# Two attention blocks on one core: loads tied to exponentials, whole products for the first values, normalisation from a copy

## The chip, the cores and the metric

The kernel runs on one core of a Trainium2 chip (trn2). The metric is the time of one execution on the device in microseconds (us); the median of three runs is given. One execution was also taken with the hardware profiler: its page and its trace are what is quoted here.

The engines are PE (TensorE; PEld are its weight loads), ACT (ScalarE), DVE (VectorE), POOL (GpSimd) and SP (SyncE, which here only issues DMAs). L776 means line 776 of the kernel. A row of the timeline gives start, duration, engine, line, operation, output and input, the count, and in brackets the idle time before it with what ended it.

## What is computed

Two multi-head attentions over 2048 tokens of width 1024 (32 heads of 32), each with its own input and weights; the outputs lie side by side.

```python
def _A_ref(x, wqkv, wo):                      # full attention
    q, k, v = split(x @ wqkv)                 # 32 heads x 2048 x 32
    p = softmax(q @ k.T * Dh ** -0.5)
    return (p @ v) @ wo

def _B_ref(x, wq, wk, wv, wo, beta):          # 4 segments of 512 with a memory
    q, k, v = x @ wq, x @ wk, x @ wv
    for s in range(4):
        p = softmax(qs @ ks.T * scale + mask)               # causal in the segment
        num, den = phi(qs) @ M, phi(qs) @ z + 1e-06          # phi(t) = t + 1 or exp(t)
        o = g * num / den + (1 - g) * (p @ vs)               # g = sigmoid(beta)
        M, z = M + phi(ks).T @ vs, z + sum(phi(ks))
    return concat(o) @ wo
```

## The kernel before

**Tiling.** Heads go in groups of four (8 groups), since four heads of 32 fill 128 rows. In attention A a unit is a group g and a block c of 256 queries; it has 32 score tiles of 512 columns. In attention B a unit is a segment s and a group j. `pack` joins two or three tiles to one exponential on ScalarE of up to 1536 columns; there are 828 of them, and their order is fixed by the list of units in `plan` (`PAIR`, `B_FIRST`, `B_STEP`, `B_GAP` say how units of A and B are mixed). Two slots of three PSUM banks (0 to 2 and 3 to 5) take the scores in turn, so the scores of exponential n wait until exponential n - 2 has left its banks. Four buffers per slot hold the results P.

**What goes around an exponential.** `plan_op` makes its scores (L761: 32-row products of keys and queries) and the exponential (L776), whose bias is a bound on the scores that is worked out from the squares of keys and queries (`guard_cols`, `guard_end`; the tile dg is a diagonal that spreads the columns' maxima by a product with ones). `plan_pv` adds P times the values (L825) and P times ones (L831, the row sums) into bank 7, the only bank for that (`OL_BANKS`). When a unit's last tile is in, `norm` and `recip_rows` on DVE transpose the row sums (L849), take the reciprocal (L856), transpose back (L858) and multiply the values' sums by it (L903, L919, L915 or L898). Projections and output products are jobs of eight products each in bank 6, the only bank for those (`X_BANKS`); their results are copied out by DVE (L979, L1174, L1193, L1207, L1303).

**The order.** The whole program is a list of operations with keys (planned times) and due times. `Prog.schedule` puts them into one order per engine by a list of costs; PE takes the scores when they are due and fills the rest with sums and jobs by rank (`HEAT`, `STICK`, `OVER`, `AHEAD`, `JOB_AT`, `DUE_SLOPE` and others). Each engine then runs its list in order and waits on semaphores.

**The start.** SP loads A's input transposed in six pieces (`X_PIECES`, L959), ScalarE's queue loads the first key and query weights. `plan_prologue` projects keys and queries of the first 512 tokens (`quarter`), which alternates keys and queries in eight steps, copies them out (L1103, L1105), squares them (L1141) and forms the first bias. The first units run in parts (`PARTS`): part 0 has the first quarter's keys, part 1 the second quarter's, part 2 the rest; each has a bias of its own, and partial sums are rescaled (L880, L884). The values of the first pair of groups are made by `job_V0`: for each of two halves (groups 0 and 1) and four quarters of tokens, 32 products of 128 columns, each as four quarter products of 32 output rows by `mm4`:

```python
def mm4(self, e, out, w, x, start, stop):
    for t in range(4):
        r = slice(32 * t, 32 * t + 32)
        ins = e.matmul(out[r], w[:, r], x, start=start, stop=stop, tile_position=(0, 32 * t), skip_group_check=True)
```

**Loads.** Weights come by `load_WA`, `load_WAv`, `load_WB`, `load_WBv`, `load_WoA`, B's input by `load_xB`, all issued by SP through `dma`. They wait only for the tile that they overwrite to be free, and for their place in SP's order.

**The end.** For the last two blocks of 256 queries of A, output products of seven of the eight groups are made ahead (`job_part`, L1382) and the eighth is added when the last unit is normalised (`job_last`, L1400, L1402), ScalarE and DVE copying two tiles each.

Of the kernel before, what the change touches and what calls it, by code (L numbers as in the profile page):

```python
# [7 lines left out]
ALU = mybir.AluOpType  # L8
AX = mybir.AxisListType

P = 128
# [3 lines left out]
D = 1024  # L15
NG = 8
NSEG = 4
L = 512
SCALE = DH ** -0.5

QC = 256
# [6 lines left out]
PAIR = ((6, 0), (6, 1), (6, 2), (7, 0), (7, 1), (7, 2), (6, 3), (6, 4), (7, 3), (7, 4), (6, 5), (7, 5), (6, 6), (7, 6), (6, 7),  # L28
# [6 lines left out]
B_FIRST, B_STEP, B_GAP = 8.5, 1.3, 3.0  # L35
B_STEP3 = 1.2
# [26 lines left out]
def mark(rs, *tag):  # L63
    for r in rs:
        r.tag = tag
# [71 lines left out]
HEAT = 0.55  # L137
STICK = 0
OVER = 0.3
# [3 lines left out]
MARGIN = 0.5  # L143
RXJ = 4
LEAD_A, LEAD_B, DUE_AT, DUE_SLOPE = 15.0, 15.0, 8.0, 0.3
# [273 lines left out]
class _Kernel:  # L419
# [34 lines left out]
    def dma(self, fn, sem, key, reads=(), writes=(), issue=0.65, lat=3.0, eng="SP"):  # L454
        return self.pg.op(eng, fn, issue, key, reads, writes, sem=sem, lat=lat)

    def build(self):
        nc = self.nc
        with ExitStack() as es:
            self.es = es  # L460
            self.alloc()
            self.items = []
            self.plan()
# [30 lines left out]
    def alloc(self):  # L494
# [16 lines left out]
        self.r_WAv = Res()  # L511
# [71 lines left out]
        self.sm_WAv = self.sem("d_WAv")  # L583
# [129 lines left out]
    def plan_op(self, take, cols, T, slot):  # L713
# [15 lines left out]
        def f(key):  # L729
# [48 lines left out]
            a.prog = True  # L778
            b = 0
# [62 lines left out]
    def recip_rows(self, src, rsrc, n, key, add=None):  # L842
# [6 lines left out]
        self.dve(lambda e: e.transpose(T1[:, 0:n], src), n, key, rsrc, [r1])  # L849
# [8 lines left out]
        self.dve(lambda e: e.transpose(T2[:, 0:n].rearrange("p (b r) -> p b r", r=32), bc), n, key, [rr], [r2])  # L858
# [8 lines left out]
    def norm(self, t, key):  # L867
# [21 lines left out]
        else:  # L889
            lsrc, ro = self.ps[:, lcol:lcol + QC], [ob]  # L890
        if kind == "A":
            T2, r2 = self.recip_rows(lsrc, ro, QC, k)
# [15 lines left out]
        else:  # L908
            T2, r2 = self.recip_rows(lsrc, ro, QC, k)
# [4 lines left out]
            if t["s"] == 0:  # L914
                self.dve(lambda e: e.scalar_tensor_tensor(out=dst, in0=osrc, scalar=gcol, in1=T2[:, 0:QC], op0=ALU.mult,  # L915
                                                          op1=ALU.mult), QC, k, [ob, r2, self.r_g], rds)
            else:
                holds(rds, "mem", t["s"])
                self.dve(lambda e: e.scalar_tensor_tensor(out=T2[:, 0:QC], in0=osrc, scalar=gcol, in1=T2[:, 0:QC], op0=ALU.mult,  # L919
                                                          op1=ALU.mult), QC, k, [ob, r2, self.r_g], [r2])  # L920
# [4 lines left out]
    def load_WA(self, g, kq, key, eng="SP"):  # L925
# [5 lines left out]
                 lat=3.5, eng=eng)  # L931

    def load_WAv(self, g2, key, eng="SP"):
        mark([self.r_WAv], "W", g2)
        src = self.A_wqkv.rearrange("(i p) n -> p i n", p=P)[:, :, 2 * D + 256 * g2:2 * D + 256 * g2 + 256]
        self.dma(lambda e: e.dma_start(self.WAv[:, :, :], src), self.sm_WAv, key, [], [self.r_WAv], lat=4.8, eng=eng,
                 )
# [117 lines left out]
    def plan_prologue(self):  # L1055
# [17 lines left out]
        def loads(key):  # L1073
            for kq in range(2):
                self.load_WA(0, kq, key, eng="ACT")
            for n, (h, lo, hi, issue, lat) in enumerate(X_PIECES):
# [4 lines left out]
                if n == 1:  # L1081
                    self.load_WAv(0, key)
# [479 lines left out]
```

## Time and profile before

| | |
|---|---|
| median of 3 runs | 1206.79 us (1205.52 to 1206.8) |
| the profiled execution | 1208.03 us, its span 1206.3 us |
| ACT busy | 1168.2 us, 97% of the span |
| PE busy | 1132.0 us, 94% |
| DVE busy | 562.1 us, 47% |
| POOL busy | 216.0 us, 18% |
| chain that ended last | ACT 58%, PE 32%, DVE 6%, issue 3% |
| DMA | 65.73 MB, mean 54 GB/s |

The span runs from the first to the last instruction. The chain that ended last is followed back from the last instruction, at each step to what released it or to the instruction before it on its engine. Matmul ends are modelled, so a busy PE need not be PE at its peak. The page's DMA line cuts the span into 40 equal slices of 30 us, each digit the busy share of the DMA engines in tenths.

### The profile page before, as it was taken

How to read it: one execution, taken by the hardware profiler on the slowest of the kernel's cores; microseconds unless marked ns; L12 is line 12 of the kernel's file. 1: busy time of each engine (PE TensorE's matmuls, PEld its weight loads, DVE VectorE, ACT ScalarE, POOL GpSimd, SP SyncE). 2: the span in 40 equal slices, each digit the busy share in tenths (PEclk: the TensorE clock that was granted, in tenths of full speed). 3: DMA queues.
4: the chain of work that ended last, by engine and by line, in shares of the span. 5: the costliest groups of instructions: out<-in, count | busy, mean ns of one | idle time of the engine just before them, and what ended most of it. 6: DMA issues, size and time to landing. Idle time of an engine off the chain costs nothing.

```text
span 1206.3 us, 54054 instructions
## 1 busy us (share of the span) xinstructions
PE 1132.0 (94%) x25352; PEld 554.6 (46%) x25352; DVE 562.1 (47%) x1268; ACT 1168.2 (97%) x868; POOL 216.0 (18%) x279
## 2 busy tenths in 40 slices
PE   7999999999999999899999999989999999988998
PEld 4455444464444444365444444544444444433444
DVE  2353444444443465645634566375425563643223
ACT  4999999999999999999999999999999999999997
POOL 1210131302120222211201331222002230100000
PEclk9999999999999999999999999999999999999999
DMA  9701331412111223103211123002022410100101
GB/s 198 190 19 43 85 77 40 85 23 64 44 33 46 64 53 80 31 7 66 64 44 33 34 66 77 17 22 48 29 75 59 146 25 7 33 20 24 38 24 46
DMA packets 162159, 65.73 MB, mean 54 GB/s; under 512 B 131728, under 2 KB 159120, under 8 KB 161936
## 3 DMA queue, kind: packets, MB, share of 16 engines
q1 hardware_dynamic: 159568, 61.50, 21.0%
q8 instruction: 198, 3.24, 1.1%
q10 hardware_dynamic: 2368, 0.79, 0.3%
q14 instruction: 25, 0.20, 0.1%
HBM read 39.00 MB, written 11.73 MB: 42 GB/s over the span
## 4 chain that ended last, share of the span: by engine, by line
ACT 58%; PE 32%; DVE 6%; issue 3%; SPq 1%; DMA 1%; DVEq 0%; ACTq 0%
ACT P L776 56%; PE ps L451 16%; PE ps L761 7%; PE ps L825 5%; PE ps L831 4%; ACT PKQ_B L1228 1%; DVE T L849 1%; SPq L959 1%; DVE PKQ_B L1233 1%; DVE T L858 1%; DMA xT_A<-in_A_x_dram 1%; DVE T L919 0%; DVE cols L1001 0%; DVE PKQ_B L1230 0%; DVE KQ_A L979 0%
## 5 line engine op out<-in xcount | busy, mean ns | idle before, releaser
L776 ACT ACTIVATE P<-ps,bias 128x1536 bf16<-128x1536 f32 (+3 forms) x828 | 1148.1, 1601 | 20.3 <-PE ps L761 10.9
L831 PE MATMUL ps<-P,onesb 128*32 128x256 bf16 (+1 forms) x4864 | 301.4, 272 | 1.2 <-issue 1.2
L761 PE MATMUL ps<-KQ_A 32*128 32x256 bf16 x4096 | 276.8, 274 | 21.1 <-ACT P L776 18.5
L825 PE MATMUL ps<-P,V_A 128*32 128x256 bf16 x4096 | 260.5, 276 | 6.3 <-ACT P L776 1.7
L761 PEld LDWEIGHTS ps<-KQ_A 32*128 32x128 bf16 x4096 | 80.9, 92 | 236.1 <-issue 123.4
L451 PE MATMUL ps<-xT_A,W_A 128*32 128x512 bf16 x2048 | 145.6, 387 | 7.2 <-DVE KQ_A L979 2.0
L451 PE MATMUL ps<-xT_B,W_B 128*32 128x512 bf16 x2048 | 145.5, 382 | 6.0 <-DVE OT_B L1254 1.3
L831 PEld LDWEIGHTS ps<-P,onesb 128*32 128x32 bf16 x4864 | 131.9, 97 | 32.0 <-issue 1.9
L825 PEld LDWEIGHTS ps<-P,V_A 128*32 128x32 bf16 x4096 | 110.0, 97 | 66.5 <-issue 33.7
L985 POOL TENSOR_TENSOR sqB<-KQ_B 128x512 bf16<-128x512 bf16 x64 | 66.9, 1045 | 368.6 <-DVE KQ_B L979 350.3
L788 POOL TENSOR_SCALAR_AFFINE_SELECT P<-P 128x768 bf16<-128x768 bf16 (+2 forms) x128 | 80.8, 654 | 253.0 <-ACT P L776 252.8
L985 POOL TENSOR_TENSOR sqA<-KQ_A 128x512 bf16<-128x512 bf16 x60 | 63.3, 1055 | 248.0 <-DVE KQ_A L979 218.6
L1303 DVE CAST outsb<-ps 128x512 bf16<-128x512 f32 x56 | 38.6, 690 | 134.7 <-PE ps L451 134.6
L849 DVE STREAM_TRANSPOSE T<-ps 128x256 f32<-128x256 f32 (+1 forms) x148 | 72.4, 489 | 59.4 <-PE ps L831 46.3
L979 DVE CAST KQ_B<-ps 128x512 bf16<-128x512 f32 x64 | 44.2, 690 | 116.3 <-PE ps L451 110.8
L979 DVE CAST KQ_A<-ps 128x512 bf16<-128x512 f32 x60 | 41.3, 688 | 102.2 <-PE ps L451 102.1
L451 PE MATMUL ps<-Wv_A,xT_A 128*32 128x256 bf16 (+1 forms) x2560 | 74.2, 252 | 5.8 <-issue 3.4
L858 DVE STREAM_TRANSPOSE T<-rc 128x256 f32<-128x256 f32 (+1 forms) x152 | 73.6, 485 | 3.9
L451 PE MATMUL ps<-Wv_B,xT_B 128*32 128x512 bf16 x1024 | 71.7, 382 | 2.9 <-DVE cols L1001 1.6
L451 PEld LDWEIGHTS ps<-xT_A,W_A 128*32 128x32 bf16 x2048 | 46.0, 96 | 60.9 <-issue 23.3
L451 PE MATMUL ps<-Wo_B,OT_B 128*32 128x512 bf16 x1024 | 72.5, 382 | 0.5 <-DVE outsb L1303 0.3
L451 PEld LDWEIGHTS ps<-xT_B,W_B 128*32 128x32 bf16 x2048 | 44.9, 96 | 56.3 <-issue 28.0
(88 smaller groups left out, 779.1 us busy)
## 6 DMA issues: line engine op xcount, KB each, us to landing
Wv_B<-in_B_wv_dram SPq DMA_DIRECT2D x8, 1024.0 KB, 5.9
W_B<-in_B_wk_dram SPq DMA_DIRECT2D x32, 256.0 KB, 3.0
W_B<-in_B_wq_dram SPq DMA_DIRECT2D x32, 256.0 KB, 3.0
out_dram<-outsb SPq DMA_DIRECT2D x56, 128.0 KB, 1.8
W_A<-in_A_wqkv_dram SPq DMA_DIRECT2D x14, 256.0 KB, 3.0
ot_a_scratch<-OTst SPq DMA_DIRECT2D x51, 64.0 KB, 1.6
xT_A<-ot_a_scratch SPq DMA_DIRECT2D x6, 512.0 KB, 7.0
Wv_A<-in_A_wqkv_dram SPq DMA_DIRECT2D x4, 512.0 KB, 4.9
```

What stands on the lines that cost most here:

```text
L451: ins = e.matmul(out[r], w[:, r], x, start=start, stop=stop, tile_position=(0, 32 * t), skip_group_check=True)
L761: ins = e.matmul(out, kap, qap, start=st, stop=True, tile_position=(32 * h, 0), skip_group_check=True)
L776: a = self.act(lambda e: e.activation(dst, src, ACT.Exp, bias=self.bias[:, bc:bc + 1], scale=SCALE), cols, key, res + [self.r_bias[bc]], [rP])
L788: self.pool(lambda e, v=v, pat=pat: e.affine_select(v, v, pattern=pat, compare_op=ALU.is_ge, fill=0.0, base=0, channel_multiplier=-1), (m ...
L825: ins = e.matmul(self.ps[32 * h:32 * h + 32, 512 * obk + q0:512 * obk + q0 + nq], vt[:, c0 + 32 * h:c0 + 32 * h + 32], Pt[:, b, off:off + nq],
L831: ins = e.matmul(self.ps[32 * h:32 * h + 32, lcol + q0:lcol + q0 + nq], self.onesb[:, 0:32], Pt[:, b, off:off + nq], start=False, stop=las ...
L849: self.dve(lambda e: e.transpose(T1[:, 0:n], src), n, key, rsrc, [r1])
L858: self.dve(lambda e: e.transpose(T2[:, 0:n].rearrange("p (b r) -> p b r", r=32), bc), n, key, [rr], [r2])
L959: return self.dma(lambda e: e.dma_start(dst, src, transpose=True), sem, key, reads, writes, issue=issue, lat=lat)
L979: self.dve(lambda e: e.tensor_copy(dst, out), ncol, key + 1.0, [self.bank[b]], rdst)
L985: self.pool(lambda e: e.tensor_tensor(sq[:, :], src, src, ALU.mult), 512, key, [rsrc], [rs], rate=0.5)
L1303: self.dve(lambda e: e.tensor_copy(ob[:, :], self.ps[:, 512 * b:512 * b + 512]), 512, key + 1.0, [self.bank[b]], [ro])
```

## The change

Seven edits:

- `dma` takes a flag `gate`. With it the DMA also waits for the last exponential whose planned time is not after the DMA's key. All weight loads, B's input, beta and B's output weights use it. The planner's cost of issuing a DMA goes from 0.65 to 0.4.
- B's first input is planned at 30 instead of 4 (`RX0`), beta at 60 instead of 20, B's output weights at 200 instead of 100.
- `job_V0` makes each product whole (128 output rows, one weight load and one matmul) instead of four quarter products; the planner knows this as a third mode of PE, "full".
- The first pair's value weights come in two halves, the second half ahead of the last piece of A's input.
- In `recip_rows` DVE copies the values' sums from PSUM to SBUF right behind the first transpose (`keep`), and the multiplication reads that copy. Partial units and the very last unit have no such copy.
- `quarter` does four steps of keys, four of queries, then again four and four.
- Constants of the planner change: the mix of units and the ranks of jobs. The changed program has the same ScalarE instructions in the same sizes, 123 more copies on DVE, and 256 whole products on PE where 1024 quarter products stood.

```diff
+PAIR = (... (6, 3), (7, 3), (6, 4), (7, 4) ...)          # was (6, 3), (6, 4), (7, 3), (7, 4)
-B_FIRST, B_STEP, B_GAP = 8.5, 1.3, 3.0
-B_STEP3 = 1.2
+B_FIRST, B_STEP, B_GAP = 10.0, 1.25, 3.0
+B_STEP3 = 1.15
...
-HEAT = 0.55
-STICK = 0
-OVER = 0.3
+HEAT = 0.6
+STICK = 0.5
+OVER = 0.4
...
-MARGIN = 0.5
+MARGIN = 1
+RX0 = 30.0
-LEAD_A, LEAD_B, DUE_AT, DUE_SLOPE = 15.0, 15.0, 8.0, 0.3
+LEAD_A, LEAD_B, DUE_AT, DUE_SLOPE = 15.0, 12.0, 8.0, 0.5
...
-    def dma(self, fn, sem, key, reads=(), writes=(), issue=0.65, lat=3.0, eng="SP"):
-        return self.pg.op(eng, fn, issue, key, reads, writes, sem=sem, lat=lat)
+    def dma(self, fn, sem, key, reads=(), writes=(), issue=0.4, lat=3.0, eng="SP", gate=False):
+        o = self.pg.op(eng, fn, issue, key, reads, writes, sem=sem, lat=lat)
+        n = bisect.bisect_right(self.exp_keys, key)
+        if gate and n:
+            o.deps.add(self.exps[n - 1])
+        return o
...
-    def recip_rows(self, src, rsrc, n, key, add=None):
+    def recip_rows(self, src, rsrc, n, key, add=None, keep=None):
...
+        if keep is not None:
+            self.dve(lambda e: e.tensor_copy(T2[:, n:2 * n], keep), n, key, rsrc, [r2])
...
+        keep = osrc if t["part"] is None and (kind, g, t["c"]) != ("A", 7, 7) else None
+        T2, r2 = self.recip_rows(lsrc, ro, QC, k, keep=keep)
+        if keep is not None:
+            osrc, ro = T2[:, QC:2 * QC], []
...
-                if n == 1:
-                    self.load_WAv(0, key)
+                if n in (1, 4):
+                    self.load_WAv(0, key, n // 4, n // 4 + 1)
...
-            for i in range(8):
-                for kq in range(2):
+            for i, kq in [(i, kq) for lo in (0, 4) for kq in range(2) for i in range(lo, lo + 4)]:
...
-        self.item(20.0, beta)
+        self.item(60.0, beta)
...
-                o = self.pe(lambda e, i=i, t=t, k=k: self.mm4(
-                    e, self.ps[:, 512 * b + P * k:512 * b + P * k + P], self.xT[:, i, P * t:P * t + P],
-                    self.WAv[:, i, P * half:P * half + P], i == 0 and k == 0, i == 7), 0.0565, key,
-                    [self.r_WAv, self.r_xT[i][c]], [self.bank[b]])
+                o = self.pe(lambda e, i=i, t=t, k=k: e.matmul(
+                    self.ps[:, 512 * b + P * k:512 * b + P * k + P], self.xT[:, i, P * t:P * t + P],
+                    self.WAv[:, i, P * half:P * half + P], start=i == 0 and k == 0, stop=i == 7, skip_group_check=True), 0.058, key,
+                    [self.r_WAv[half], self.r_xT[i][c]], [self.bank[b]], mode="full")
...
-        self.item(100.0, lambda key: self.dma(... self.WoB ... lat=12.0))
+        self.item(200.0, lambda key: self.dma(... self.WoB ... lat=12.0, gate=True))
...
-                end, rx = 10.0, 4.0
+                end, rx = 10.0, RX0
...
-                r = max(en["B", s - 1, 4 * hh + 3] + 12.0, rx + 12.0) if s else 16.0
+                r = max(en["B", s - 1, 4 * hh + 3] + 12.0, rx + 12.0) if s else rx + 12.0
```

More of the change, by code (lines that the diff above doesn't have):

```diff
@@ L778, in f @@
             a.prog = True
+            self.exps.append(a)
+            self.exp_keys.append(key)
             b = 0
@@ L1176, in job_V0 @@
     def job_V0(self, half, c, key, bank=None, behind=None, copy_behind=None):
-        holds([self.r_WAv], "W", 0)
+        holds([self.r_WAv[half]], "W", 0)
         holds([r[c] for r in self.r_xT], "x")
```

51 lines of the change are left out of this document (25 added, 26 removed).

## The prediction

> **What bounds the kernel now.** I read the page first, then ScalarE's instructions in order of time, then PE and DMA where ScalarE idles, then how the built program of the change stands on each engine.
>
> ```profile
> span 1206.3 us, 54054 instructions
> PE 1132.0 (94%) x25352; PEld 554.6 (46%) x25352; DVE 562.1 (47%) x1268; ACT 1168.2 (97%) x868; POOL 216.0 (18%) x279
> DMA  9701331412111223103211123002022410100101
> q8 instruction: 198, 3.24, 1.1%
> ```
>
> ScalarE is busy for 1168.2 of 1206.3 us, nearly all of it in 828 exponentials. The changed program has the same ScalarE instructions in the same sizes, so the change can move only its 38.1 us of idle time. Here is most of that (in brackets the idle time before a row, and what ended it):
>
> ```profile
> 15.14 3.17 ACT L776 ACTIVATE P<-ps,bias 128x1536 bf16<-128x1536 f32 x2 [3.57 <-PE ps L451]
> 19.05 5.08 ACT L776 ACTIVATE P<-ps,bias 128x1536 bf16<-128x1536 f32 x4 [0.73 <-PE ps L761]
> 26.52 1.54 ACT L776 ACTIVATE P<-ps,bias 128x1536 bf16<-128x1536 f32 x1 [2.40 <-PE ps L451]
> 31.06 1.54 ACT L776 ACTIVATE P<-ps,bias 128x1536 bf16<-128x1536 f32 x1 [1.39 <-PE ps L761]
> 34.37 1.54 ACT L776 ACTIVATE P<-ps,bias 128x1536 bf16<-128x1536 f32 x1 [1.77 <-PE ps L761]
> 36.09 11.74 ACT L776 ACTIVATE P<-ps,bias 128x1536 bf16<-128x1536 f32 x8 [0.18 <-PE ps L761]
> ...
> 70.41 26.78 ACT L776 ACTIVATE P<-ps,bias 128x1536 bf16<-128x1536 f32 x19 [1.73 <-PE ps L831]
> 98.30 2.97 ACT L776 ACTIVATE P<-ps,bias 128x1536 bf16<-128x1536 f32 x2 [1.12 <-PE ps L761]
> ...
> 101.47 7.38 ACT L776 ACTIVATE P<-ps,bias 128x1536 bf16<-128x1536 f32 x5 [0.20 <-PE ps L761]
> 109.25 1.54 ACT L776 ACTIVATE P<-ps,bias 128x1536 bf16<-128x1536 f32 x1 [0.40 <-PE ps L761]
> 110.96 1.54 ACT L776 ACTIVATE P<-ps,bias 128x1536 bf16<-128x1536 f32 x1 [0.17 <-PE ps L761]
> 113.10 8.79 ACT L776 ACTIVATE P<-ps,bias 128x1536 bf16<-128x1536 f32 x6 [0.59 <-PE ps L761]
> ...
> 449.17 6.84 ACT L776 ACTIVATE P<-ps,bias 128x1536 bf16<-128x1536 f32 x5 [1.19 <-PE ps L761]
> 478.95 1.54 ACT L776 ACTIVATE P<-ps,bias 128x1536 bf16<-128x1536 f32 x1 [0.72 <-PE ps L761]
> 481.53 1.54 ACT L776 ACTIVATE P<-ps,bias 128x1536 bf16<-128x1536 f32 x1 [1.04 <-PE ps L761]
> ...
> 516.82 25.22 ACT L776 ACTIVATE P<-ps,bias 128x1536 bf16<-128x1536 f32 x19 [0.37 <-PE ps L761]
> ...
> 1085.30 10.70 ACT L776 ACTIVATE P<-ps,bias 128x1536 bf16<-128x1536 f32 x8 [0.36 <-PE ps L761]
> 1096.79 100.17 ACT L776 ACTIVATE P<-ps,bias 128x1536 bf16<-128x1536 f32 x72 [0.79 <-PE ps L831]
> 1201.71 1.08 ACT L1400 ACTIVATE KQ_B<-ps 128x512 bf16<-128x512 f32 x2 [4.75 <-PE ps L451]
> ```
>
> About 15 us pass before the first exponential and 9 after the last; 10.7 lie in the gaps shown up to 113 us, and 4.5 in those shown after it. Each gap ends on PE. PE's rows at the early ones:
>
> ```profile
> 13.14 1.07 PE L451 MATMUL ps<-Wv_A,xT_A 128*32 128x128 bf16 x64
> 14.03 0.39 PE L451 MATMUL ps<-dg,onesf 128*32 128x128 f32 x8
> 26.29 1.95 PE L451 MATMUL ps<-Wv_A,xT_A 128*32 128x128 bf16 x126
> 30.45 0.23 PE L451 MATMUL ps<-Wv_A,xT_A 128*32 128x128 bf16 x2 [2.21 <-issue]
> 69.73 0.29 PE L825 MATMUL ps<-P,V_A 128*32 128x256 bf16 x4 [0.49 <-DVE V_A L1193]
> 97.20 0.29 PE L831 MATMUL ps<-P,onesb 128*32 128x256 bf16 x4 [1.21 <-issue]
> 108.21 0.23 PE L451 MATMUL ps<-Wv_A,xT_A 128*32 128x128 bf16 x2 [0.73 <-issue]
> 30.70:34.20 3.50, 2.95 (x32) 0.90 (x32) 0.69 (x1) 1.54 (x1) 0.00 (x0) 0.65 1.25 275
> 444.60:448.10 3.50, 3.46 (x74) 2.23 (x78) 2.63 (x7) 3.38 (x3) 0.00 (x0) 0.52 0.19 37
> ```
>
> "issue" is time for which PE waited on nothing recorded, and it lies in or just behind the first pair's value products (L451, Wv_A, 128 columns). These use four quarter products for each whole one: 128 matmuls and 128 weight loads in 1.95 us. The 3.24 MB of the instruction queue over 50,704 PE instructions are 64 bytes each, its 198 packets 256 instructions each, so that stretch eats one packet in 1.95 us. I read the stalls as late instructions. The last two rows are windows (third number from the end: granted clock): after a stretch in which PE does little, the clock falls to about half for some 3.4 us, and ScalarE gaps (34.37, 449.17) follow.
>
> **The change part by part.** I count exponentials from 0.
>
> *Whole products, late bias.* In the order of before, half of the first value job stands ahead of the bias sum (dg) and half behind it; in the changed order all 32 whole products stand ahead. If a whole product takes what four quarters take, 1.07 / 16 = 67 ns, they end at 13.14 + 2 x 1.07 = 15.28. The first exponential stood 15.14 - 14.03 = 1.11 behind dg, so it starts at 16.4, 1.25 late. The six exponentials of the first quarter last 3.17 + 5.08 = 8.25, to 24.6. The next bias sum is queued behind scores 7, which wait for exponential 5 to free its banks: 0.35 for the scores, 1.11 for the chain, so exponential 6 starts near 26.1 instead of 26.52: **-0.4**. Keys ahead of queries bring the keys' copy out four products earlier and let it run beside the queries' products; that takes one copy of 512 columns (an estimate of 0.7, from 0.42 for 256 columns in a row below) off the chain whose bias sum started at 26.52 - 1.11 = 25.4, so its column is ready near 24.7, 0.3 before scores 7 let it through. So that edit is worth nothing while scores 7 cover it, and its absence about 0.4.
>
> For the whole product's price I take 67 ns because the same bits are streamed; the bounds are half of it (which gains 0.3, since the next column is then late) and 67 plus a wholly exposed 128-column weight load:
>
> ```profile
> L761 PEld LDWEIGHTS ps<-KQ_A 32*128 32x128 bf16 x4096 | 80.9, 92 | 236.1 <-issue 123.4 <-ACT P L776 108.7 <-DVE V_A L1193 0.4
> ```
>
> 67 + 92 = 159 ns makes 5.1 us for 32: exponential 0 at 19.3, and exponential 10 three to four us later than below. [...] No run here shows whole products yet.
>
> *The stall behind exponential 7.* The value job of the second quarter falls from 256 instructions to 64, a quarter packet; I let the 2.21 us stall go, and with it the half clock behind it. Exponentials 8, 9, 10 then follow without the gaps of 1.39, 1.77 and 0.18: **-3.3**. What is late next: 32 x 67 ns = 2.1 us of products before scores 8, which the two exponentials ahead (26.78 / 19 = 1.4 each) cover.
>
> *70 us.* The exponential at 70.41 waits for a value-sum of exponential 25, which in before stands behind scores 33 and a value copy; in the changed order it stands ahead of scores 32, and beta's casts are no longer between. **-1.5** of 1.73.
>
> *97 to 113 us.* Gaps of 1.12, 0.20, 0.40, 0.17 and 0.59, all beside the remaining quarter-product jobs: 2.48 in all, **-2.2**, leaving 0.3 for PE's mode changes.
>
> *Gated loads.* Every load of weights and second input now waits on SP for a named exponential; stores and transposes behind it in SP's queue wait too, which their rings of three and four buffers bear. Counting exponentials between a load's gate and its first product in PE's order, the time to spare is 3.1 us at the least and mostly 5 to 15, against:
>
> ```profile
> DMA to landing us min/median/max: 2.8/3.0/7.8
> ...
> 212.41 5.18 SPq L959 DMA_TRANSPOSE xT_B<-in_B_x_dram  x1
> 218.25 0.43 SPq L950 DMA_DIRECT2D Wv_B<-in_B_wv_dram  x1
> Wv_B<-in_B_wv_dram SPq DMA_DIRECT2D x1, 1024.0 KB, 7.8
> Wv_B<-in_B_wv_dram SPq DMA_DIRECT2D x8, 1024.0 KB, 5.9
> ```
>
> (first row: W_B loads after 60 us; the last two: value weights, that of 218.25 and the median of all). One place does not fit. At exponential 180 the second segment's input and its 1 MB of value weights are released together, and the key weights follow behind them, wanted ahead of scores 190, about 9.1 us after the gate. Issue of the input takes 5.2, so the value weights go at 5.8 and land at 11.7 to 13.6, the key weights behind them at about 12 to 14.5. ScalarE is fed until 12.0 if they land by 11.1, so it loses 0.8 to 3.5 there, and PE, idle for some 4 us, gets the half clock behind it, about 0.8 more. Bounds 0.5 and 5; I take **+2.5**. Before the change this input came with 49 exponentials to spare.
>
> *The rest up to the end.* Light stretches in PE's order (five exponentials with PE's sums and products under about a third of the time) stood at exponentials 295, 335, 685, 745 and 820 in before; the gaps at 449, 516 and 1085 to 1096 us lie right behind three of them. After the change, other than 185, they stand at 412, 508, 546, 590 and 817. About as many: 4.5 us of gaps become 3.7, **-0.8**, with bounds of 3 on both sides. In this lies the extra copy:
>
> ```profile
> L849 DVE STREAM_TRANSPOSE T<-ps 128x256 f32<-128x256 f32 x124 | 55.3, 446 | 47.3 <-PE ps L831 46.3
> ...
> 1199.94 0.42 DVE L898 TENSOR_TENSOR xT_A<-ps,T 128x256 bf16<-128x256 f32 x1
> ```
>
> The second row reads the same tile as the copy will: 123 copies of about 0.42 us are 52 us more on DVE, 51% of the span, beside other work. The one bank of sums is freed after transpose and copy, 0.9 us, instead of a full chain of about 1.6; but DVE's copies of other products queue 0.4 longer. Zero, bounds 1.5 either way.
>
> *The end.* Behind the last scores nine partial output products stand no longer. The last normalised column (the row just shown) was ready at 1200.36, ScalarE's closing copies began at 1201.71. PE spent the 1.35 us between on four partial products and the first two closing ones; the four go, two thirds of it: **-0.9**. The stores behind move along.
>
> Sum: -0.4 -3.3 -1.5 -2.2 +2.5 -0.8 -0.9 = -6.6. The profiled execution took 1208.03, its span 1206.3 and 1.7 around it; it becomes 1201.4. The median of the runs shown is 1206.79, 1.24 lower, and becomes 1200.2.
>
> **The rivals.** *A, the stalls stay.* [...] By a mechanism of this kernel: if the stalls come from DMA traffic or from the array and not from the count of instructions, 3.3 and 2.2 stay and the time is 1205.7. Against it: the idle of 2.21, 1.21 and 0.73 stands in or right behind the dense jobs, and the last two at 97 and 108 us, in the fourth slice of the page, where DMA is busy to one tenth. [...] Chance 0.12.
>
> *B, slower: late weights.* 17 weight loads have under 6.4 us to spare; one exponential of 1.4 us more is covered. At the 3.0 us median none but the one above is late. If the gate pushes loads behind stores and transposes so that 7 us is usual (7.8 was seen), they are late by 32 us in all, 11 of it past the cover, and the time is 1200.2 + 11 = 1211. It decides from landings of about 6.5 us, where some 6 are lost and the gain is gone. For it: 7.8 exists; against: the median. Chance 0.10.
>
> *C, exposed weight loads.* At 159 ns the first stage gives about 4 back: 1204.2. Chance 0.08.
>
> **How the numbers follow.** My forecast has 0.70. A measurement tells this kernel from no change at about 0.2%, 2.4 us. Faster (under 1204.4): nearly all of the forecast's range and half of C and a little of A, 0.77. Same: most of A, the rest, 0.12. Slower: B and an ill turn of the middle, 0.11. The range adds the bounds of the unknown terms (3 for the dips, 2.5 for the late weights, 1.5 for DVE): 1194.5 down, and up across C and A to 1206.5.
>
> **What would show it.** Right: exponential 0 near 16.4, exponential 10 near 32 instead of 36.09; no "issue" idle over 0.5 us beside Wv_A; no gap from 60 to 113 us over 0.5; a gap of 1 to 4 us near 285 to 295 us with PE waiting for a W_B load; last copies on ScalarE within 4 us of the last exponential; DVE near 615 us. Wrong: stalls of the old size in the first 113 us, PE waits for W_B in many places, more than six windows of half clock, or a first exponential past 18.

## The result, and the profile after

The changed kernel takes 1191.47 us (median of 4 runs, 1190.54 to 1192.79) against 1206.15 us for the kernel before on the same chip (4 runs, 1204.25 to 1206.8): ratio 0.9882, 95% interval 0.9865 to 0.9899. That is 14.7 us faster. 6.6 had been forecast, and the result lies below the range. From the page after (total, busy times, instruction queue, chain of work that ended last by engine):

```profile
span 1188.8 us, 52631 instructions
PE 1130.3 (95%) x24584; PEld 549.5 (46%) x24584; DVE 590.4 (50%) x1391; ACT 1164.2 (98%) x868; POOL 218.4 (18%) x279
q8 instruction: 192, 3.15, 1.1%
ACT 69%; PE 24%; DVE 3%; issue 2%; DMA 1%; POOL 0%; ACTq 0%; DVEq 0%; SPq 0%; POOLq 0%
```

The span fell by 17.5 us (from 1206.3). In medians it is 14.7, because the profiled execution of before (1208.03) lay 1.9 above its median and that of after (1190.54) 0.9 below. ScalarE's part in the last chain rose from 58% to 69%, PE's fell from 32% to 24%. ScalarE's rows with idle time of over 0.3 us ahead of them, of the whole timeline after the first exponential:

```profile
16.39 7.85 ACT L784 ACTIVATE P<-ps,bias 128x1536 bf16<-128x1536 f32 x6 [4.63 <-DVE bias L1063]
25.74 1.54 ACT L784 ACTIVATE P<-ps,bias 128x1536 bf16<-128x1536 f32 x1 [1.51 <-PE ps L1198]
27.36 17.28 ACT L784 ACTIVATE P<-ps,bias 128x1536 bf16<-128x1536 f32 x12
44.63 62.33 ACT L784 ACTIVATE P<-ps,bias 128x1536 bf16<-128x1536 f32 x44
...
286.92 11.78 ACT L784 ACTIVATE P<-ps,bias 128x1536 bf16<-128x1536 f32 x9 [1.35 <-PE ps L769]
...
1184.14 1.08 ACT L1412 ACTIVATE KQ_B<-ps 128x512 bf16<-128x512 f32 x2 [3.39 <-PE ps L453]
```

Behind exponential 6 there is no such gap for 260 us (the third and fourth row, without brackets, show a stretch of it); of the gaps from 30 to 113 us nothing is left. The one new gap is at 286.92, the place named in the prediction.

**Waits that no gap shows.** ScalarE's busy time fell too, from 1168.2 to 1164.2, though it does the same work. The rows tell why: one exponential of 1536 columns lasts 1.54, two last 2.97 (in a row of before), so the next one starts 1.43 after the first, while that is still on record. A wait of under 0.1 us is thus counted as busy. So I measure lateness from start to start: over all ScalarE instructions, the distance to the next start less the one it has when nothing is late (in these traces 1.423 us for 1536 columns, 1.21 for 1280, 0.996 for 1024, 0.783 for 768, 0.946 and 0.519 for copies of 1024 and 512). Summed over stretches of exponentials, from the traces ("first at" is the start of exponential 0; the names in the left column are the experiments further down):

| kernel | first at | 0-10 | 11-60 | 61-179 | 180-199 | 200-826 | to the closing copies | sum |
|---|---|---|---|---|---|---|---|---|
| before | 15.14 | 7.49 | 6.42 | 1.87 | 0.23 | 12.84 | 5.08 | 33.9 |
| after | 16.39 | 1.69 | 0.07 | 1.44 | 1.88 | 6.48 | 3.58 | 15.1 |
| e1, quarters again | 16.04 | 3.18 | 6.98 | 1.97 | 1.74 | 8.62 | 3.52 | 26.0 |
| e2, whole in before | 15.51 | 2.91 | 2.57 | 1.66 | 0.23 | 11.56 | 5.02 | 24.0 |
| e4, no copy | 16.39 | 1.63 | 0.00 | 1.59 | 5.54 | 16.73 | 3.83 | 29.3 |
| e7, old mix | 16.53 | 1.69 | 2.55 | 1.43 | 0.20 | 12.18 | 4.59 | 22.6 |
| e9, three parts in before | 15.55 | 4.48 | 0.80 | 1.38 | 0.16 | 7.73 | 3.52 | 18.1 |
| e10, copy, old order | 15.14 | 8.83 | 6.80 | 2.82 | 0.69 | 24.42 | 5.02 | 48.6 |
| e13, whole and copy | 15.38 | 3.79 | 2.65 | 1.60 | 0.50 | 9.63 | 3.52 | 21.7 |
| e14, whole and mix | 15.61 | 4.58 | 0.72 | 1.40 | 0.47 | 16.61 | 3.68 | 27.5 |
| e16, nudge | 16.26 | 1.72 | 0.11 | 1.12 | 7.01 | 9.55 | 3.52 | 23.0 |
| e17, nudge, values behind | 16.06 | 1.71 | 0.08 | 1.03 | 2.15 | 9.24 | 3.51 | 17.7 |

The sums give the spans: 33.9 - 15.1 - 1.25 (later first exponential) = 17.5. These are single executions. Four with one order of the engines (after, e1, e3, e8) have 6.5, 8.6, 6.9 and 8.8 in the stretch 200-826, so a difference of 2 there says nothing.

### The profile page after: what moved, and what is told of

Read it like the earlier page. It is cut to its first block, busy times and chain, and to the rows that moved or that the text cites. A ratio compares the mean times of both kernels' runs of the same rounds, so it can differ in the third digit from the quotient of the medians.

```text
span 1188.8 us, 52631 instructions
## 1 busy us (share of the span) xinstructions
PE 1130.3 (95%) x24584; PEld 549.5 (46%) x24584; DVE 590.4 (50%) x1391; ACT 1164.2 (98%) x868; POOL 218.4 (18%) x279
## 3 DMA queue, kind: packets, MB, share of 16 engines
q1 hardware_dynamic: 160608, 61.50, 21.7%
## 4 chain that ended last, share of the span: by engine, by line
ACT 69%; PE 24%; DVE 3%; issue 2%; DMA 1%; POOL 0%; ACTq 0%; DVEq 0%; SPq 0%; POOLq 0%
ACT P L784 67%; PE ps L453 12%; PE ps L769 5%; PE ps L835 4%; PE ps L841 3%; ACT PKQ_B L1240 2%; DMA xT_A<-in_A_x_dram 1%; DMA W_B<-in_B_wk_dram 0%; DVE T L859 0%; POOL P L798 0%; DVE OT_B L1266 0%; DVE T L861 0%; PE ps L1198 0%; DVE PKQ_B L1245 0%; DVE outsb L1315 0%
## 5 line engine op out<-in xcount | busy, mean ns | idle before, releaser
L453 PE MATMUL ps<-xT_A,W_A 128*32 128x512 bf16 x2048 | 141.4, 382 | 3.8 <-DVE OT_B L1266 1.3
L798 POOL TENSOR_SCALAR_AFFINE_SELECT P<-P 128x768 bf16<-128x768 bf16 (+2 forms) x128 | 83.6, 675 | 258.0 <-ACT P L784 254.2
L453 PE MATMUL ps<-Wv_A,xT_A 128*32 128x256 bf16 x1536 | 55.5, 275 | 1.8 <-DVE OT_B L1266 1.4
```

The lines of the kernel that those rows point to most:

```text
L798: self.pool(lambda e, v=v, pat=pat: e.affine_select(v, v, pattern=pat, compare_op=ALU.is_ge, fill=0.0, base=0, channel_multiplier=-1), (m ...
```

## The experiments

### Whole or quarter products (e1, e2)

e1 puts the quarter products back into the changed kernel; e2 puts whole ones into the kernel before. Neither changes the order on any engine.

```diff
-                o = self.pe(lambda e, i=i, t=t, k=k: e.matmul(..., skip_group_check=True), 0.058, key, ...   # e1
+                o = self.pe(lambda e, i=i, t=t, k=k: self.mm4(...), 0.058, key, ...
```

> The changed kernel with the first pair's values as four quarter products each again, everything else and the order of every engine unchanged. Theory 1 (the early stalls came from the many short instructions of the quarter products, 128 matmuls and 128 weight loads in about 1.95 us): the idle stretches that nothing explains, of 0.5 to 2.2 us, are back beside Wv_A in the first 113 us, and the time is 1197 to 1200 us, 6 to 8 above the changed kernel. Theory 2 (they came from weights and B's input that were loaded at the start beside the exponentials, which the gates now hold back): no such stretch over 0.5 us, and 1190 to 1193 us.

> The kernel before with whole products for the first pair's values, its order unchanged and its loads ungated. Theory 1 (instruction count): the unexplained idle stretches in the first 113 us go, and the time is 1196 to 1200 us, 6 to 10 below the kernel before. Theory 2 (traffic of the loads at the start): the stretches stay, 1205 to 1207.5 us.

e1 took 1199.8 us (ratio to before 0.9958, 0.9943 to 0.9974), 8.3 above the changed kernel; e2 1198.91 (0.9951, 0.9933 to 0.997), 6.0 below the kernel before. From e1, two rows of PE's waits (total, times, longest), and PE and ScalarE behind one of its value jobs:

```profile
PE ps L453 <- issue: 5.3, 4, 2.2
PE ps L769 <- issue: 2.1, 1, 2.1
...
58.54 0.55 PE L769 MATMUL ps<-KQ_A 32*128 32x256 bf16 x6 [2.06 <-issue]
59.13 3.06 ACT L784 ACTIVATE P<-ps,bias 128x1536 bf16<-128x1536 f32 x2 [1.73 <-PE ps L769]
```

7.4 us of "issue" are back, at other places than in before, and ScalarE waits behind them. In the changed kernel PE's waits have none of this kind, in e2 two, of 0.6 and 0.5 us. Theory 1 holds: without the short instructions the stalls of the first 113 us go, also in e2, which leaves the loads ungated.

Two things in the traces go further than the two theories. The length of a stall went with the traffic: in the five traces with these quarter products (before, e1, e5, e10, e18), the stalls of 0.4 us and more in the first 113 us lasted 1.23 to 3.01 us where the DMA engines' share in the 2 us ahead was 0.79 or more, and 0.40 to 1.24 where it was at most 0.46 (in before 2.21 at a share of 1.15, 1.21 at 0.44, 0.73 at 0.03). So the loads may still decide how long a stall is; no run changed the traffic alone under quarter products. And the values of the later groups are still made of quarter products (of 256 columns), with stalls behind them of 1.33 us in e14 (at 748.40) and 2.45 in e15. Whether the stalls are instruction fetches was not measured itself; instruction packets go with them (192 after, 198 in before and in e1).

### Gates, and the late weights at 285 us (e3, e8)

e3 leaves all orders as changed but drops the waits of loads for exponentials. e8 plans the 1 MB value load later, so that SP issues W_B ahead of it.

```diff
+            self.pg.schedule(); [o.deps.discard(x) for o, x in self.gates]                 # e3
-            self.item(rx + 0.1, lambda key, s=s: self.load_WBv(s, 0, key))                  # e8
+            self.item(rx + (5.0 if s else 0.1), lambda key, s=s: self.load_WBv(s, 0, key))
```

> The changed kernel without the waits of the loads for an exponential, the order of every engine unchanged. Theory 1 (the gates matter little, and cost at the place near 285 us where W_B lands late): the loads near exponential 180 still stand in one order on SP, so 1190 to 1192 us, at best 1 to 2 us below the changed kernel, and the gap before PE's first product with W_B (1.33 us) gets smaller. Theory 2 (the gates are what removed the early stalls): 1196 to 1200 us, with unexplained idle stretches beside Wv_A. Theory 3 (the gates keep transfers from slowing ScalarE or PE in the middle of the span): 1193 to 1197 us, with no unexplained idle stretches at the start.

> The changed kernel with the load of B's first value weights (1 MB) planned 5 us later for segments 1 to 3, so that on SP the loads of W_B stand ahead of it; PE, DVE, ScalarE and GpSimd keep their orders. Theory S (W_B lands late at 285 us because the 1 MB load is ahead of it on the same queue): W_B lands within 3.5 us of its issue, PE's wait of 1.33 us for it goes, the three windows at half clock from 279 to 289 us go or shrink, and the time is 1188.5 to 1190.5 us, 1 to 3 below the changed kernel. Rival P (PE simply comes to that product too early, and the output store that stands at SP's head until 277 us sets the time): W_B still lands at 284 us or later, and 1191 to 1192.5 us.

e3: 1194.16 us (0.9907, 0.989 to 0.9925). e8: 1190.74 us (0.9883, 0.9864 to 0.9902). SP in the changed kernel (start, duration of the issue), PE's wait there, and size and time from issue to landing of that W_B load:

```profile
272.60 3.75 SPq L972 DMA_TRANSPOSE xT_B<-in_B_x_dram  x1
277.04 0.32 SPq L922 DMA_DIRECT2D ot_a_scratch<-OTst  x1
277.41 0.43 SPq L963 DMA_DIRECT2D Wv_B<-in_B_wv_dram  x1
278.35 1.61 SPq L972 DMA_TRANSPOSE PKt_B<-PKQ_B  x1
280.07 0.51 SPq L957 DMA_DIRECT2D W_B<-in_B_wk_dram  x1
285.23 1.05 PE L453 MATMUL ps<-xT_B,W_B 128*32 128x512 bf16 x8 [1.33 <-DMA W_B<-in_B_wk_dram]
W_B<-in_B_wk_dram SPq DMA_DIRECT2D x1, 256.0 KB, 5.1
```

And in e3 without gates:

```profile
265.06 5.95 SPq L972 DMA_TRANSPOSE xT_B<-in_B_x_dram  x1
277.29 0.32 SPq L922 DMA_DIRECT2D ot_a_scratch<-OTst  x1
277.65 0.95 SPq L963 DMA_DIRECT2D Wv_B<-in_B_wv_dram  x1
...
279.95 0.59 SPq L957 DMA_DIRECT2D W_B<-in_B_wk_dram  x1
286.09 1.04 PE L453 MATMUL ps<-xT_B,W_B 128*32 128x512 bf16 x8 [2.15 <-DMA W_B<-in_B_wk_dram]
W_B<-in_B_wk_dram SPq DMA_DIRECT2D x1, 256.0 KB, 6.1
```

The input now goes 7.5 us earlier, but W_B still only at 279.95: at SP's head stands a store that waits for its data until 277. So the gate does not make W_B late; the queue behind that store does, and the 1 MB issued ahead of it: W_B lands 5.1 us after its issue here and 6.1 in e3, against 3.3 in e8. The first half of my expectation (the gap gets smaller) was wrong: it grew. Theory 2 falls as well, as no stall came back. The time is in theory 3's range, but the trace puts nearly all of the loss at this one place (stretch 180-199: 3.59 against 1.88) and not in the middle. What the gates are worth, 2.7 us by the medians, 1.9 by the two spans, is not sure: the intervals overlap. e8 confirms theory S for the place: W_B lands in 3.3 us there, PE does not wait, and the stretch 180-199 falls from 1.88 to 0.21. But the time did not fall measurably; it lies between the two forecasts. In part that is this (windows of e8: length, busy time and instructions of PE, PEld, DVE, ACT, POOL, granted clock, DMA share, GB/s):

```profile
1166.20:1169.60 3.40, 2.37 (x40) 0.90 (x38) 0.90 (x3) 3.40 (x3) 0.00 (x0) 0.87 0.11 39
1169.60:1173.00 3.40, 3.40 (x56) 1.35 (x52) 0.69 (x1) 2.35 (x3) 0.00 (x0) 0.63 0.02 5
```

And of the changed kernel, whose PE does the same there about 1 us later:

```profile
1166.20:1169.60 3.40, 1.78 (x38) 0.68 (x36) 1.82 (x6) 3.40 (x4) 0.00 (x0) 1.00 0.14 48
1169.60:1173.00 3.40, 3.40 (x76) 1.59 (x72) 0.69 (x1) 3.40 (x4) 0.00 (x0) 1.00 0.02 5
```

Behind this light stretch of PE (2.37 of 3.40 us busy in e8, 1.78 in the changed kernel) the granted clock was 0.63 in e8, where ScalarE loses 1.05, and 1.00 in the changed kernel. Why it fell in the one and not in the other no run shows.

### The copy of the values' sums (e4, e5, e10)

e4 takes the copy out of the changed kernel and e5 puts it into the kernel before; both let the planner order anew. e10 puts it into the kernel before with every other instruction in its old place.

```diff
-        keep = osrc if t["part"] is None and (kind, g, t["c"]) != ("A", 7, 7) else None    # e4
+        keep = None
...
+            c = Op("DVE", lambda e, dst=dst, src=src: e.tensor_copy(dst, src), 0.39, 0.1, t1.key)    # e10
+            q.insert(i + 1, c)
+                if o.pvn is not None and m in o.deps:
+                    o.deps.discard(m)
+                    o.deps.add(c)
```

> The changed kernel without the copy of the values' sums: the multiplication reads bank 7 again, and the planner orders with that. Theory K (the bank that comes free earlier is what removed the small late scores between 110 us and the end, some 6 to 7 us in the two profiled executions): 1196 to 1199 us, PE waits again for DVE's multiplication and transposes before value sums, and the windows at half clock in the middle return. Theory R (the planner's constants did that): 1190 to 1193 us, DVE's busy time down by 20 to 50 us from 590.

> The kernel before with the copy of the values' sums alone (its planner orders anew with it; quarter products, old constants, no gates). Theory K (the copy frees bank 7 earlier, and that by itself takes away the late scores in the middle): 1196 to 1201 us, 4 to 9 below the kernel before, with the early stalls still there. Theory I (the copy pays only with the changed constants and mix, which without it lost 13 us): 1203 to 1207 us.

> The kernel before with the copy of the values' sums put behind the first transpose on DVE, all other instructions in the order of before on every engine: only the next unit's first value sum waits for the copy instead of the multiplication. Theory D (the copy's worth is direct, PE waited for bank 7): 1199 to 1203 us. Theory O (the copy's worth is in the order that the planner can make with it): 1204 to 1206.5 us, no more than 1 us from the kernel before.

e4: 1204.42 us (0.9992, 0.9981 to 1.0003), 13 above the changed kernel. e5: 1201.97 (0.998, 0.9966 to 0.9994), 3.4 below the kernel before and between the two forecasts. e10: 1221.88 (1.013, 1.0107 to 1.0152), 16 slower, which neither theory had. PE's waits in e10 (total, times, longest):

```profile
PE ps L451 <- DVE cols L1030: 8.3, 14, 1.1
PE ps L451 <- DVE KQ_A L1008: 6.0, 11, 1.6
PE ps L451 <- DVE KQ_B L1008: 5.0, 11, 0.7
PE ps L451 <- DVE outsb L1332: 3.7, 7, 1.1
```

The same waits in the kernel before:

```profile
PE ps L451 <- DVE cols L1001: 5.2, 13, 0.6
PE ps L825 <- DVE T L919: 3.5, 8, 0.7
PE ps L451 <- DVE KQ_A L979: 3.3, 6, 1.3
PE ps L451 <- DVE KQ_B L979: 2.7, 7, 0.6
PE ps L451 <- DVE outsb L1303: 1.8, 5, 0.6
```

The wait for the multiplication (L919) is gone in e10, as meant. But 0.39 us more on DVE for each of 123 units delays the copies that empty the one bank of the jobs, and these four waits grow from 13.0 to 23.0. All waits of PE for DVE of over 0.15 us rise from 31.5 to 47.5 us, as much as the kernel loses; with the order of the changed kernel they are 19.6, and 35.6 without the copy (e4). So in the order of before the early release of bank 7 is worth less than the copy costs. Taking the copy out of the changed order as it stands was not tried.

### Old ranks, old mix (e6, e7)

```diff
-HEAT = 0.6 ; STICK = 0.5 ; OVER = 0.4 ; MARGIN = 1 ; LEAD_B = 12.0 ; DUE_SLOPE = 0.5     # e6
+HEAT = 0.55 ; STICK = 0 ; OVER = 0.3 ; MARGIN = 0.5 ; LEAD_B = 15.0 ; DUE_SLOPE = 0.3
-B_FIRST, B_STEP, B_STEP3 = 10.0, 1.25, 1.15 ; PAIR = (... (6, 3), (7, 3), (6, 4), (7, 4) ...)    # e7
+B_FIRST, B_STEP, B_STEP3 = 8.5, 1.3, 1.2 ; PAIR = (... (6, 3), (6, 4), (7, 3), (7, 4) ...)
```

> The changed kernel with the planner's rank constants of before (HEAT, STICK, OVER, MARGIN, LEAD_B, DUE_SLOPE), all else as changed. Theory R (the ranks carry part of the gain in the middle): 1194 to 1199 us, with more windows at half clock. Theory K (the copy carries it): 1190 to 1193.5 us.

> The changed kernel with the mix of units of before (PAIR, B_FIRST, B_STEP, B_STEP3). Theory M (when units of B stand among those of A decides where scores come late): 1194 to 1199 us. Theory K (the copy carries the middle, whatever the mix): 1190 to 1193.5 us.

e6: 1191.35 us (0.989, 0.987 to 0.9909): the ranks carry nothing that shows. e7: 1198.03 (0.9945, 0.9925 to 0.9965), 6.6 above the changed kernel. Part of it lies at a place known from before (PE and ScalarE of e7; the sum at 65.46 is what exponential 32, at 65.79, waits for):

```profile
62.08 1.96 PE L1198 MATMUL ps<-Wv_A,xT_A 128*128 128x128 bf16 x32
64.79 0.39 PE L769 MATMUL ps<-KQ_A 32*128 32x256 bf16 x6 [0.42 <-ACT P L784]
65.46 0.28 PE L841 MATMUL ps<-P,onesb 128*32 128x256 bf16 x4
65.79 2.97 ACT L784 ACTIVATE P<-ps,bias 128x1536 bf16<-128x1536 f32 x2 [1.05 <-PE ps L841]
```

And PE of the changed kernel at the same two steps:

```profile
61.80 0.28 PE L841 MATMUL ps<-P,onesb 128*32 128x256 bf16 x4
...
62.23 0.39 PE L769 MATMUL ps<-KQ_A 32*128 32x256 bf16 x6
```

With the old mix the gap near 66 to 70 us is there again, though the products are whole and beta's casts are gone: the sum stands behind a whole value job and behind scores 33 (64.79), as in before. In the changed kernel the same sum stands ahead of scores 32 (62.23), and nothing waits. The old mix has the gap in e2 (1.63 us at 65.89) and e13 too; with the new mix the sum stands ahead and the gap is gone, with and without the copy (e4, e9, e14).

### Which parts make up the gain (e9, e13, e14)

All three are the kernel before with whole products and one or both of the copy and the new mix: no gates, old ranks, old first loads.

> The kernel before with three parts of the change alone: whole products, the copy of the values' sums, and the new mix of units. No gates, old rank constants, old order and times of the first loads, keys and queries alternating. Theory 3 (these three are the whole gain): 1190.5 to 1194 us. Rival G (the gates, the ranks and the times of the loads carry some of it beside them): 1196 us or more.

> The kernel before with whole products and the copy, with the old mix. Theory S (parts add up: whole products some 6, the copy some 3): 1195 to 1197 us. Theory J (copy and mix gain only together): 1198 to 1200 us, as with whole products alone.

> The kernel before with whole products and the new mix of units, without the copy. Theory S (the mix is worth some 6 us by itself): 1191 to 1194 us. Theory J (without the copy the new mix costs, as the changed kernel without the copy showed): 1201 to 1206 us.

| the kernel before with | us | ratio, interval |
|---|---|---|
| whole products (e2) | 1198.91 | 0.9951, 0.9933 to 0.997 |
| the copy (e5) | 1201.97 | 0.998, 0.9966 to 0.9994 |
| whole products, copy (e13) | 1196.17 | 0.9923, 0.9909 to 0.9937 |
| whole products, mix (e14) | 1202.15 | 0.9975, 0.9965 to 0.9984 |
| whole products, copy, mix (e9) | 1192.74 | 0.9896, 0.9883 to 0.991 |
| all (the changed kernel) | 1191.47 | 0.9882, 0.9865 to 0.9899 |

Whole products (6.0) and the copy (3.4) add up: 9.6 together. The mix costs about 3 without the copy (e14 against e2) and gains about 3 with it (e9 against e13). Theory S is right for the copy, theory J for the mix, as far as these orders go. Where e14 loses, from its ScalarE:

```profile
679.66 1.06 ACT L1228 ACTIVATE PKQ_B<-KQ_B 128x1024 bf16<-128x1024 bf16 x1 [3.65 <-PE ps L451]
```

These three parts have 12.9 of the 14.7; the rest is within the intervals. It is a balance more than nothing: in e9 exponential 6 starts at 27.70, in the changed kernel at 25.74, but the changed kernel loses 1.7 at the late weights, which e9 does not. e9 also lacks an edit that the list ahead of the prediction does not name: the change raises the planner's fixed cost of a transpose to 0.17 us and that of the multiplications of B to 0.2.

How sure are the single terms? Whole products were changed with every order kept, in both directions (e1, e2). The copy and the mix were judged with a new order each time, and the nudges below, which change no work, move the time by 1.3 and 5.8. The copy is faster in each of four pairs (e5 and before, e13 and e2, e9 and e14, the changed kernel and e4), by 2.7 to 13; the new mix is slower in one pair (e14 and e2) and faster in two (e9 and e13, the changed kernel and e7). So it is shown that the three make the gain together (e9), and that the copy helps once the order is made anew; how much of the 3 us of each is the order that came with it is not. Of the 13 that e4 loses, 3.7 are at the late weights (stretch 180-199: 5.54 against 1.88), where PE waits 3.18 us for W_B.

With the copy (e5, e13, e9) or with the new mix (e14) the closing copies come 3.5 to 3.7 late, without both 5.0 (before, e2). That this too depends on the order show e4 (3.83), e7 (4.59) and e10 (5.02).

### Keys ahead of queries, and a try at a faster version (e11, e12)

e11 goes back to `for i in range(8) for kq in range(2)`; e12 has the constants of e6 and the load of e8.

> The changed kernel with keys and queries alternating in each quarter again, all else unchanged. If keys ahead of queries are worth nothing, since the score products before them end later anyway: 1190.5 to 1192.5 us, exponential 6 starts at 25.7 us as before. If they matter: exponential 0 or 6 starts 0.4 us or more later and the time rises with it.

> The changed kernel with the old rank constants and the 1 MB value load behind W_B (the two parts that cost nothing or a little by themselves), a try at a faster version. If the wait for W_B, which cost 2.4 us in the profiled run with the old ranks, is the only thing that joins them: 1188.5 to 1190 us. If the time that is won there is lost again at later places: 1190 to 1192 us.

e11: 1191.26 us (0.9879, 0.9866 to 0.9892), so that edit is worth nothing. e12: 1190.03 (0.9868, 0.9853 to 0.9883), the fastest kernel tried, but not surely apart from the changed one. The time lies at the border of its two forecasts.

### How much hangs on the exact order (e15 to e18)

```diff
-B_FIRST, B_STEP, B_GAP = 10.0, 1.25, 3.0      # e15
+B_FIRST, B_STEP, B_GAP = 10.0, 1.28, 3.0
-    def dve(self, fn, n, key, reads=(), writes=(), rate=0.96, fixed=0.12):      # e16; e17 with e8's load; e18 in before
+    def dve(self, fn, n, key, reads=(), writes=(), rate=0.96, fixed=0.13):
```

> The changed kernel with B_STEP at 1.28 instead of 1.25, nothing else. Theory F (the new mix is better as such, a little off it is about as good): 1190 to 1194 us. Theory L (the values of the mix are one well-fitting order among many, and a neighbour loses what it won): 1195 to 1203 us.

> The changed kernel with the planner's fixed cost of a DVE instruction at 0.13 instead of 0.12 us: no part of the work is changed, the planner only makes a somewhat other order. Theory F (the parts of the change make the gain, whatever the exact order): 1190.5 to 1193 us. Theory L (one well-fitting order among many): 1194 us or more.

> The nudged order (the planner's fixed cost of a DVE instruction at 0.13) with the 1 MB value load planned 5 us later, behind W_B; PE, DVE, ScalarE and GpSimd keep the nudged order. Theory W (the nudge lost its 5.8 us for the most part at one place, where PE waits 4.55 us for W_B behind the value load at 286 us): that wait goes to under 1 us and the time is 1191.5 to 1193.5 us. Theory L (the loss is spread over the order): 1194.5 us or more.

> The kernel before with the same nudge of the planner (0.13 instead of 0.12 us), no part of the change. If the kernel before is one order among many of much the same worth: 1200 to 1211 us, away from 1205.8 by over 1 us either way. If its order is about what its parts give: within 1 us of the kernel before.

e15: 1204.85 us (0.9991, 0.9979 to 1.0004): nearly all is lost. e16: 1197.28 (0.9927, 0.9915 to 0.9939), 5.8 lost. e17: 1192.68 (0.9888, 0.9872 to 0.9904), 4.6 of it back. e18: 1204.87 (0.9985, 0.9973 to 0.9997), 1.3 below the kernel before, as the first of its two forecasts has it, but barely. e16 at the known place:

```profile
286.21 0.62 PE L453 MATMUL ps<-xT_B,W_B 128*32 128x512 bf16 x4 [4.55 <-DMA W_B<-in_B_wk_dram]
287.42 1.54 ACT L784 ACTIVATE P<-ps,bias 128x1536 bf16<-128x1536 f32 x1 [4.11 <-PE ps L769]
```

And e17, in which only the value load went behind W_B:

```profile
282.18 0.62 PE L453 MATMUL ps<-xT_B,W_B 128*32 128x512 bf16 x4 [0.84 <-DMA W_B<-in_B_wk_dram]
283.45 1.54 ACT L784 ACTIVATE P<-ps,bias 128x1536 bf16<-128x1536 f32 x1 [0.46 <-PE ps L769]
```

Theory W holds: the nudge lost most of its time at one place, and with the load out of the way the nudged order is as good as the changed one within 1.2 us. Theory L is right for e15, whose ScalarE waits for scores at two places where neither kernel of the comparison has a gap (the row of PE stands ahead of the first):

```profile
798.11 0.61 PE L769 MATMUL ps<-KQ_A 32*128 32x256 bf16 x5 [2.45 <-issue]
798.82 1.54 ACT L784 ACTIVATE P<-ps,bias 128x1536 bf16<-128x1536 f32 x1 [2.57 <-PE ps L769]
...
965.66 5.85 ACT L784 ACTIVATE P<-ps,bias 128x1536 bf16<-128x1536 f32 x4 [3.34 <-PE ps L769]
```

The second stands behind a wait of PE for W_B (2.17 us), the first behind the stall at quarter products named under e1. With the exponential behind the first they hold 7.5 of the 12 us that e15 is later than the changed kernel in the stretch 200-826 (18.5 against 6.48); its closing copies come another 3.5 later (7.1 against 3.58), and the rest is spread. So a few places can spoil an order; the change's values of the mix meet few of them. How many orders are as good was not tried.

## Why the prediction was wrong, step by step

The direction, the early mechanism and the two places of new waits (late bias, late weights) were right. The sum was too small by 10.9 us of span: 3.5 in the early terms, 6.0 in the middle, 0.9 in the late weights, 0.6 at the end. The lower end of the range, 1194.5, does not follow from the three bounds that it names (1200.2 - 3 - 2.5 - 1.5 = 1193.2); the result lies below either. Three rows of the profile after for what follows, the first whole products on PE, the group of their weight loads, and that of the copies on DVE (busy us, mean ns):

```profile
13.42 1.96 PE L1198 MATMUL ps<-Wv_A,xT_A 128*128 128x128 bf16 x32
...
L1198 PEld LDWEIGHTS ps<-Wv_A,xT_A 128*128 128x128 bf16 x256 | 14.3, 98 | 4.1 <-issue 3.0 <-DVE cols L1058 0.3 <-DVE bias L1063 0.2
L861 DVE COPY T<-ps 128x256 f32<-128x256 f32 x123 | 48.2, 392 | 0.1
```

- **Late bias (-0.4, measured -0.8).** The 32 products took 1.96 us, 61 ns each with the last one's tail and 56 from start to start, against 1.07 / 16 = 67 taken for them. Rival C (159 ns) falls. Exponential 0 came at 16.39 as forecast, 6 at 25.74 instead of 26.1. With the old ranks (e6) exponential 0 starts at 15.3 and 6 still at 25.7, so the first start costs nothing. Keys ahead of queries: 0, as said (e11).
- **Stall behind exponential 7 (-3.3, measured -3.8).** Right, cause too (e1, e2): exponentials 7 to 18 follow without a gap. Rival A falls, though the traffic that it names may set the length of a stall. That the stalls are late instructions was my estimate and is not shown: the runs show that stalls of 2 us come and go with the number of instructions in a dense stretch (2.2 us in before and e1, with 128 quarter products in 1.95 in before; no wait on "issue" in the changed kernel, with 32 whole ones in 1.96), and not what part their fetch has in them.
- **70 us (-1.5, measured -2.8 for exponentials 11 to 33).** Right in sign, and right for the value sum: it stands ahead of scores 32 wherever the gap is gone and behind scores 33 wherever it is there (after, e4, e9 and e14 against before, e2, e7 and e13). The absent casts did not do it, since they are absent in e7 too. What moved the sum is the mix of units (e7, e9, e14).
- **97 to 113 us (-2.2, measured -3.5).** Right in cause: 3.58 in before, 0.24 with whole products alone (e2), 0.06 after. Of the 0.3 left for PE's mode changes no run shows a sign.
- **Gated loads (+2.5, measured +1.65).** Place and size were near, the cause half: the 1 MB ahead of the keys was in the forecast and holds (e8, e17), but that the gate sets the time does not. Without the gate the wait is longer (2.15 us in e3 against 1.33), and W_B is issued 0.12 us earlier (279.95 against 280.07), because of the store at SP's head. Of the 0.8 that the forecast has for half clock behind PE's wait no run shows a part of its own; the clock records have half the clock from 279.02 to 289.26 us, so from before that wait (283.90 to 285.23) on. Rival B falls: no other load came late by over 0.5 us in the changed kernel.
- **The rest up to the end (-0.8, measured -6.8).** This is the step that failed. I counted light stretches in PE's order, found "about as many", and let 4.5 us of gaps become 3.7. None of the five places named (412, 508, 546, 590, 817) shows a late exponential of over 0.3 us in the trace after. The 4.5 us of gaps fell to 0.4 (0.17 at 772.61, 0.23 at 1073.38) and not to 3.7, and they were only the visible part: from start to start before lost 14.7 in exponentials 61 to 179 and 200 to 826, after 7.9. Over the same stretches the table gives 13.2 with whole products (e2), 11.2 with the copy too (e13) and 9.1 with the mix too (e9), each step no larger than the scatter of single traces. By the clock records, windows at half clock between 113 us and the last exponential fell from four in before (444.73, 478.86, 513.00, 1083.02) to one after other than those at 279 us (736.41); the forecast had about as many. But e14 has none there and is late by 16.6, so the clock is not the whole of it. The copy was put at 0 within 1.5 either way by weighing DVE's load against the earlier release at a fixed order. At a fixed order it is in fact far worse (e10, +16); with the order made anew the time is 3.4 lower in the old mix (e5), and the new mix pays only beside it (9.4 between e14 and e9). I priced an edit by its instructions where the time hung on the order made with it; how much of that worth is the copy's and how much is luck of the order stays open.
- **The end (-0.9, measured -1.5).** Right in sign. DVE was forecast at 615 us and is at 590.4: the copies are 48.2 us by their group's row, near the 52 counted, but their records overlap others (added singly, DVE's records rise from 595.9 to 647.5).

## What to carry to other kernels

Where many short instructions stand close together on PE, count instructions as well as bits: beside jobs of 128 quarter products (1.95 us) stood stalls of 0.40 to 3.01 us here (before, e1, e5, e10, e18), and none beside 32 whole ones (1.96 us, the changed kernel). In a kernel whose order a planner makes, an edit's worth can't be read from its own instructions: test it at the fixed order and with the order made anew, and nudge the planner once, to see how much of a difference belongs to the order alone. Lateness of a saturated engine is better summed from start to start than read from gaps, and when one load is late, look at what stands ahead of it in its queue before blaming the wait that was added to it.

## What was not expected of the hardware

- A stream of whole 128-column products with weights loaded for each ran at 1.96 us for 32 in the changed kernel, where its weight loads, 98 ns each in their group's row, would make 3.1 alone. In the records they overlap: the 256 loads are 14.3 us busy, 25.1 added singly.
- The clock records of the two profiles before the last exponential have half the clock for 3.413 us at 31.72, 444.73, 478.86, 513.00 and 1083.02 us in before, and for 10.24 us at 279.02 and 3.413 at 736.41 in the changed kernel. In the 3.40 us ahead of these PE was busy for 0.72 to 2.17 us, but it was for 1.78 too in the changed kernel from 1166.20 to 1169.60, and the clock behind that was 1.00.
- 256 KB of weights landed 3.3 and 3.6 us after their issue where the 1 MB value load was issued behind them (e8, e17), 5.1 to 6.7 where it was issued ahead of them (after, e3, e16).
